# Twelve products of constants on TensorE, ahead of five stages of an attention prologue

## The chip, the cores and the metric

One core of a Trainium2 chip. The metric is the device time of one execution in microseconds (us), taken as the median of the runs. Five engines work side by side and meet through semaphores: PE (matrix products; the trace calls its weight loads PEld), DVE and POOL (elementwise work), ACT (activations and copies) and SP, which here only issues DMAs. Each runs its own instructions strictly in the order in which they were written.

## The reference

Eight batches of 576 tokens, eight heads of 64. Heads 0 to 3 attend to the last 32 tokens, heads 4 to 7 to every 32nd token back. The result, 8 x 576 x 512, goes through a layer norm and a two-layer network of width 2048 with a ReLU, and is added to itself:

```
scores = scale * np.matmul(q, k.transpose(0, 1, 3, 2))
mask_local = (rel >= 0) & (rel < stride)
mask_strided = (rel >= 0) & (pos[None, :] % stride == pos[:, None] % stride)
...
attn = np.exp(scores - np.max(scores, axis=-1, keepdims=True))
attn = attn / (np.sum(attn, axis=-1, keepdims=True) + 1e-09)
x = np.matmul(attn, v) ... reshape(B, S, H * D)
xn = (x - mu) / np.sqrt(var + 1e-06) * g_ln
out = x + np.maximum(xn @ w_ch1, 0.0) @ w_ch2
```

## The kernel before

**Tiling.** The 8 x 576 tokens are cut into nine chunks of 512; chunk c is the first 512 tokens of batch c, and the ninth holds the last 64 of each batch. The network runs chunk by chunk over sixteen slices f of 128 hidden columns. For each slice PE makes a hidden tile `ph` (`ffn1_high` L748 and `ffn1_low` L755, twelve products of 512 columns) and then four output tiles `po` (`ffn2` L775, twelve more), which collect over the slices. Data and weights are each split into a high and a low part, so that three fast products stand for one exact one. Attention runs in pairs of heads and is spread between the slices: while chunk c is in the network, the pairs of batch c + 1 are worked on.

**The prologue** has no chunk to hide behind. It does batch 0 (four pairs), starts batch 1, prepares the sixteen weight slices, and feeds the network of chunk 0 as soon as a slice is ready. Its order is written out by hand in the string `ORDER`, one word for each step, of the form `op:k:i:buf`; `one()` looks the word up and issues the instructions. Since every engine runs in written order, the string is the schedule. The words that matter here, for a pair k:

- `T` (`t_rows`, L371) turns loaded rows of q or k by products with the identity, `c` copies them out on ACT;
- `S` (`s_blocks`, L445) makes the scores, `mask` (L473) and `max` (L486) run on DVE, `sub` (L491) on POOL, `exp` (L497) on ACT;
- `PP` (`p_turn`, L501) turns the weights of attention, `pt` (L506) copies them on ACT, `V` (`v_full`, L515) multiplies by v, `den` and `xo` (L565) divide on DVE;
- `X` (L636) turns the result, `xh` (ACT) and `xl` (DVE) split it; `tp` (L415, L416, L420) turns the q and k of a later pair on DVE.

For a weight slice f: `W` issues its two loads of 512 KB on SP; `low`, `sc`, `mg`, `sg` decode it; `byg` (L270) and `add` (L275, L277) run on POOL, `cm` (L281) is one fp32 product on PE, `cen` (L284) subtracts on DVE; `hi` (L294, ACT) and `lo` (L298, POOL) split it; `F` and `H` are the two halves of `ph`, `Fb` the piece of `F:0` that waits for the last pair, `G` is `po`.

**PSUM.** Each of the prologue's words that needs a PSUM tile takes one of three pairs of banks, named by `buf` (`room()`), and waits there for the reader of the tile before. `ph` has a bank of its own. At the start `wake`, a tile in that bank, receives six products of a constant tile with itself, which nothing reads (L128).

fp32 products other than the turns of `PP` and `X` show in the trace as two records each; the turns and the network's products as one. So `S` of 24 products shows as x48.

Of the kernel before, what the change touches and what calls it, by code (L numbers as in the profile page):

```python
# [20 lines left out]
T:0:0:0 T:0:1:1 c:0:0: c:0:1: T:1:0:2 S:0::0 c:1:0: T:1:1:2 mask:0 max:0 T:2:1:0 c:1:1: sub:0  # L21
S:1::1 c:2:1: exp:0 T:2:0:2 mask:1 max:1 PP:0::0 c:2:0: T:3:0:1 sub:1 pt:0 c:3:0: V:0::2 exp:1
vs:1 S:2::0 den:0 xo:0 PP:1::1 mask:2 X:0::2 pt:1 max:2 W:0 T:3:1:0 xh:0 sub:2 V:1::1 xl:0 c:3:1:
S:3::2 den:1 r:4 xo:1 low:0:0 sc:0:0 low:0:1 exp:2 mg:0:0 mask:3 PP:2::1 X:1::0 pt:2 sg:0:0 W:1
max:3 xh:1 V:2::2 sc:0:1 xl:1 sub:3 tp:4 byg:0 exp:3 W:2 PP:3::0 add:0 den:2 S:4::1 pt:3 mg:0:1
vs:3 xo:2 cm:0::0 low:1:0 X:2::2 W:3 mask:4 sg:0:1 V:3::1 xh:2 max:4 sc:1:0 cen:0 sub:4 xl:2 r:5
hi:0:0 lowA:2:0 mg:1:0 hi:0:1 lo:0:0 F:0 exp:4 den:3 sg:1:0 lowA:3:0 lo:0:1 xo:3 sc:1:1 low:1:1
byg:1 X:3::1 mg:1:1 v:4 sg:1:1 add:1 PP:4::2 xh:3 sc:2:0 xl:3 cm:1::0 mg:2:0 Fb:0 pt:4 lowA:3:1
W:4 cen:1 H:0 lowA:2:1 sg:2:0 hi:1:0 tp:5 byg:2 V:4::0 hh:0 sc:2:1 add:2 hl:0 S:5::1 hi:1:1 st:1
mg:2:1 lo:1:0 cm:2::2 sg:2:1 F:1 W:5 mask:5 sc:3:0 lo:1:1 hi:2:1 cen:2 H:1 mg:3:0 hi:2:0 G:0  # L30
sg:3:0 hh:1 den:4 W:6 sc:3:1 hl:1 lowA:4:1 mg:3:1 lo:2:0 byg:3 lowA:4:0 F:2 sg:3:1 add:3 xo:4
sc:4:0 hi:3:1 W:7 mg:4:0 H:2 lo:2:1 lowA:5:0 sg:4:0 cm:3::0 G:1 cen:3 byg:4 sc:4:1 hi:3:0 mg:4:1
add:4 hh:2 sg:4:1 st:4 hl:2 sc:5:0 X:4::0 lo:3:0 F:3 mg:5:0 xh:4 r:6 lo:3:1 lowA:5:1 xl:4 H:3
sg:5:0 cm:4::0 hh:3 G:2 cen:4 byg:5 sc:5:1 hl:3 lowA:6:1 v:5 add:5 mg:5:1 hi:4:0 sg:5:1 lowA:6:0
lo:4:0 F:4 max:5 sc:6:0 lowA:7:0 mg:6:0 sub:5 lowA:7:1 cm:5::0 sg:6:0 H:4 cen:5 W:8 sc:6:1 byg:6
G:3 hh:4 mg:6:1 add:6 hi:4:1 hl:4 hi:5:0 sg:6:1 lo:5:0 cm:6::0 sc:7:0 F:5 cen:6 W:9 exp:5 lo:4:1
mg:7:0 hi:5:1 sg:7:0 H:5 tp:6 byg:7 sc:7:1 PP:5::0 lowA:8:0 G:4 add:7 st:0 hh:5 hi:6:0 hl:5 lo:5:1
pt:5 r:7 mg:7:1 hi:6:1 S:6::0 lo:6:0 sg:7:1 lowA:9:0 lowA:8:1 F:6 mask:6 sc:8:0 max:6 cm:7::0
mg:8:0 sg:8:0 sub:6 H:6 st:3 G:5 hh:6 cen:7 byg:8 st:2 hl:6 hi:7:0 lo:6:1 tp:7 sc:8:1 hi:7:1
V:5::0 add:8 lowA:9:1 r:8 F:7 mg:8:1 sg:8:1 lo:7:0 den:5 sc:9:0 xo:5 H:7 mg:9:0 sg:9:0 cm:8::0  # L40
hh:7 G:6 exp:6 byg:9 hl:7 W:10 sc:9:1 cen:8 add:9 mg:9:1 hi:8:0 PP:6::0 hi:8:1 sg:9:1 lo:8:0 F:8
tp:8 pt:6 W:11 lo:7:1 hi:9:1 cm:9::0 H:8 lo:8:1 sc:10:0 cen:9 lowA:10:0 G:7 lowA:10:1 mg:10:0 W:12
hi:9:0 sg:10:0 hh:8 byg:10 sc:10:1 hl:8 S:8::0 lowA:11:0 lo:9:0 mg:10:1 F:9 lowA:11:1 sg:10:1 v:6
add:10 mask:8 sc:11:0 H:9 mg:11:0 lo:9:1 lowA:12:1 sg:11:0 cm:10::0 G:8 hh:9 cen:10 byg:11 W:13
sc:11:1 hi:10:0 mg:11:1 hi:10:1 lo:10:0 hl:9 lowA:12:0 S:7::0 sg:11:1 add:11 sc:12:0 F:10 mask:7
W:14 lo:10:1 mg:12:0 cm:11::0 sg:12:0 H:10 max:7 sc:12:1 byg:12 G:9 hh:10 cen:11 st:5 add:12
mg:12:1 hi:11:0 hl:10 lowA:13:1 W:15 lo:11:0 sg:12:1 hi:11:1 cm:12::0 F:11 max:8 sc:13:0 lowA:13:0
cen:12 H:11 mg:13:0 hi:12:0 v:7 sg:13:0 lo:12:0 X:5::0 hh:11 G:10 xh:5 lo:11:1 sc:13:1 xl:5
lowA:14:1 hl:11 sub:7 hi:12:1 mg:13:1 V:6::0 lowA:14:0 r:9 byg:13 F:12 sg:13:1 den:6 add:13 xo:6
sc:14:0 H:12 lo:12:1 lowA:15:0 mg:14:0 exp:7 cm:13::0 sg:14:0 G:11 hi:13:1 cen:13 byg:14 xr:0  # L50
# [14 lines left out]
def kernel(  # L65
# [127 lines left out]
    v_l = [v_local(const.tile([P, 4 * NL, D1], F32, name="v_l")),  # L193
           v_local(early.tile([P, 4 * NL, D1], F32, name="v_l1"))]
    v_s = [v_strided(const.tile([P, 2 * NS, D1], F32, name="v_s")),
           v_strided(early.tile([P, 2 * NS, D1], F32, name="v_s1"))]


# [604 lines left out]
    for p in first:  # L803
        if p.k in BY_DVE:
            p.load_qk(early.tile([P, 2 * S], F32, name=f"raw{p.id}"))
        elif p.k == 0:
            for i in range(2):
                p.load_rows(i, nc.sync, slice(0, 1))
                p.load_rows(i, nc.scalar, slice(1, 2))
        else:  # L810
            p.load_rows(0, nc.sync)
            p.load_rows(1, nc.scalar)
    nc.sync.dma_start(gcol, g_ln.rearrange("(c p) -> p c", p=P))
    for p in first:
        p.load_v(once=True)

# [211 lines left out]
```

## Time and profile before

| | |
|---|---|
| runs | 906.57 us median of 3 (906.55 to 910.79) |
| profiled execution: span from first to last instruction | 907.3 us |
| mean granted TensorE clock over the span | 0.992 |
| PE busy | 884.9 us (98%), 7606 products |
| PEld, DVE, ACT, POOL busy | 728.8, 435.4, 199.7, 147.9 us |
| DMA | 102.98 MB, mean 114 GB/s |

The profiled execution has no time outside its span on record; its span stands 0.7 us above the median of the runs. The page divides the span into 40 slices of 22.7 us; the prologue's first 60 us, with which this document deals, are less than three of them, so the views read below are the timeline and tables of busy time over short windows.

### The profile page before, as it was taken

The page shows a single profiled execution, that of the slowest core. Times are in us where ns is not written, and L with a number is a line of the kernel's source. Part 1 is how long each engine was busy: PE and PEld are TensorE (multiplying, and loading weights), DVE is VectorE, ACT ScalarE, POOL GpSimd, SP SyncE. Part 2 cuts the span into 40 slices and gives each one's busy share as a digit, 9 for nine tenths or more (in the row PEclk, how much of TensorE's full clock was granted, in tenths as well). Part 3 has the DMA queues.
Part 4 walks back from the last instruction along what each step waited for, and adds up shares of the span by engine and source line. Part 5 has one row for each costly group of instructions (what it writes and reads, how often), then busy time and mean ns, then how long its engine had stood idle before and what let it go on. Part 6 is the DMA issues. An engine that isn't in the chain of part 4 may idle for free.

```text
span 907.3 us, 18531 instructions
## 1 busy us (share of the span) xinstructions
PE 884.9 (98%) x7606; PEld 728.8 (80%) x7606; DVE 435.4 (48%) x864; ACT 199.7 (22%) x326; POOL 147.9 (16%) x186
## 2 busy tenths in 40 slices
PE   7699999999999999999999999999999999999997
PEld 6578787888888888888888888888888888888885
DVE  2888877544654455445644464445533321132113
ACT  3477663111111111111111111111111111111110
POOL 5477774000100011000100010001000000000000
PEclk8999999999999999999999999999999999999999
DMA  8887886675867575766666665757443230002001
GB/s 166 226 257 179 247 196 114 147 111 119 134 142 109 102 137 120 124 91 141 109 134 93 135 104 141 100 127 124 116 85 91 49 128 0 1 1 93 0 1 47
DMA packets 339621, 102.98 MB, mean 114 GB/s; under 512 B 276944, under 2 KB 331344, under 8 KB 339536
## 3 DMA queue, kind: packets, MB, share of 16 engines
q1 hardware_dynamic: 249920, 85.53, 42.9%
q10 hardware_dynamic: 89616, 16.26, 11.5%
q8 instruction: 60, 0.98, 0.5%
q14 instruction: 25, 0.20, 0.1%
HBM read 74.02 MB, written 27.72 MB: 112 GB/s over the span
## 4 chain that ended last, share of the span: by engine, by line
PE 93%; DMA 2%; DVE 1%; issue 1%; SPq 1%; POOL 1%; ACT 0%; DVEq 0%; POOLq 0%; ACTq 0%
PE po L775 42%; PE ph L748 28%; PE ph L755 14%; PE m L515 2%; PE m L445 2%; DMA s<-in_moe_w_ch_dram 1%; PE t L371 1%; PE s L445 1%; DMA rows<-in_q_dram 1%; PE av L515 1%; SPq L351 1%; PE cm L281 1%; PE px L636 0%; PE pp L501 0%; POOL r L270 0%
## 5 line engine op out<-in xcount | busy, mean ns | idle before, releaser
L775 PE MATMUL po<-w,hh 128*128 128x512 f32 x1152 | 359.2, 393 | 0.0
L765 DVE SCALAR_TENSOR_TENSOR hl<-ph,hh 128x512 fp32r<-128x512 f32 x144 | 99.3, 690 | 367.0 <-ACT hh L760 367.0
L775 PEld LDWEIGHTS po<-w,hh 128*128 128x128 f32 x1152 | 213.4, 188 | 44.8
L748 PE MATMUL ph<-xh,w 128*128 128x512 f32 x576 | 226.0, 392 | 1.4 <-ACT w L294 1.2
L775 PE MATMUL po<-w,hl 128*128 128x512 f32 x576 | 224.5, 390 | 0.0
L748 PE MATMUL ph<-xl,w 128*128 128x512 f32 x576 | 224.5, 390 | 0.0
L760 ACT ACTIVATE hh<-ph 128x512 fp32r<-128x512 f32 x144 | 86.1, 598 | 483.7 <-PE ph L755 469.0
L755 PE MATMUL ph<-xh,w 128*128 128x512 f32 x576 | 155.3, 392 | 0.0
L748 PEld LDWEIGHTS ph<-xh,w 128*128 128x128 f32 x576 | 108.3, 188 | 24.1 <-ACT w L294 1.4
L775 PEld LDWEIGHTS po<-w,hl 128*128 128x128 f32 x576 | 108.1, 188 | 23.1
L755 PEld LDWEIGHTS ph<-xh,w 128*128 128x128 f32 x576 | 108.2, 189 | 22.5 <-POOL w L298 0.2
L748 PEld LDWEIGHTS ph<-xl,w 128*128 128x128 f32 x576 | 108.3, 188 | 22.0
L491 POOL TENSOR_TENSOR sm<-sm,mx 128x648 f32<-128x648 f32 (+1 forms) x32 | 40.6, 1269 | 440.4 <-DVE mx L486 440.4
L723 POOL TENSOR_TENSOR rs<-rs,mhalf 128x1 f32<-128x1 f32 x36 | 19.7, 548 | 286.5 <-DVE rs L722 286.5
L497 ACT ACTIVATE sm<-sm 128x648 f32<-128x648 f32 (+1 forms) x32 | 23.8, 742 | 104.3 <-POOL sm L491 104.3
L298 POOL TENSOR_TENSOR w<-r,w 128x512 fp32r<-128x512 f32 x32 | 41.1, 1297 | 7.3 <-ACT w L294 6.9
L687 DVE TENSOR_TENSOR xl<-xo,xh 128x512 fp32r<-128x512 f32 x24 | 16.6, 692 | 38.8 <-ACT xh L686 38.8
L686 ACT ACTIVATE xh<-xo 128x512 fp32r<-128x512 f32 x24 | 15.2, 632 | 62.0 <-DMA pd<-sm 18.2
L486 DVE TENSOR_REDUCE mx<-sm 128x12 f32<-128x648 f32 (+1 forms) x32 | 26.3, 822 | 2.1
L565 DVE TENSOR_TENSOR xo<-m,den 64x64 f32<-64x64 f32 (+3 forms) x120 | 27.1, 289 | 0.0
L781 DVE SCALAR_TENSOR_TENSOR x<-po,rs,x 128x512 f32<-128x512 f32 x36 | 24.5, 737 | 2.0 <-PE po L775 1.8
L718 DVE BATCH_NORM_STATS2 st<-x 128x6 f32<-128x512 f32 x36 | 24.3, 674 | 0.0
(95 smaller groups left out, 561.0 us busy)
## 6 DMA issues: line engine op xcount, KB each, us to landing
s<-in_moe_w_ch_dram SPq DMA_DIRECT2D x32, 512.0 KB
out_dram<-x SPq DMA_DIRECT2D x32, 256.0 KB
raw<-in_q_dram SPq DMA_DIRECT2D x112, 72.0 KB
raw<-in_k_dram SPq DMA_DIRECT2D x112, 72.0 KB
xds<-xo SPq DMA_DIRECT2D x32, 162.0 KB
v_l<-in_v_dram SPq DMA_DIRECT2D x32, 144.0 KB
pd<-sm SPq DMA_DIRECT2D x44, 96.0 KB
pt<-pd ACTq DMA_DIRECT2D x44, 96.0 KB
```

The costliest lines, as they stand in the source:

```text
L298: nc.gpsimd.tensor_tensor(out=t[:, 1], in0=self.w[i], in1=t[:, 0].bitcast(F32), op=ALU.subtract)
L445: nc.tensor.matmul(o, lhsT, rhs, start=True, stop=True, tile_position=(64 * h, pos))
L486: nc.vector.reduce_max(mx[:, :, 0:nt], sm, axis=AX.X)
L491: nc.gpsimd.tensor_tensor(out=sm, in0=sm, in1=mx[:, :, 0:nt].unsqueeze(3).broadcast_to([P, 2, nt, sm.shape[3]]), op=ALU.subtract)
L515: nc.tensor.matmul(at(h, t)[m * j:m * (j + 1)], self.p_cols(rows, t, j), self.v[rows, n, 0:w], start=True, stop=True, tile_position=(64 * ...
L565: nc.vector.tensor_tensor(out=xo[r, t0:t1, h0:h1].rearrange("p t h d -> p h t d"), in0=av, in1=den[r, h0:h1, t0:t1].unsqueeze(3).broadcast_to(
L748: nc.tensor.matmul(ph, w1h[:, cc], x[:, cc, :], start=(new and n == 0 and i == 0), stop=False)
L755: nc.tensor.matmul(ph, w1l[:, cc], xt[c][0][:, cc, :], start=False, stop=(cc == NCC - 1))
L760: nc.scalar.activation(out=hh, in_=ph, func=AF.Relu)
L765: nc.vector.scalar_tensor_tensor(out=hl, in0=ph, scalar=0.0, in1=hh.bitcast(F32), op0=ALU.max, op1=ALU.subtract)
L775: nc.tensor.matmul(po[i], hx[:, cs], w, start=(f == 0 and n == 0), stop=(f == NFC - 1 and n == 2))
L781: nc.vector.scalar_tensor_tensor(out=x, in0=po[i], scalar=rs, in1=x, op0=ALU.mult, op1=ALU.add)
```

## The change

The string `ORDER` gets a new word `Z`, five times:

```diff
-T:0:0:0 T:0:1:1 c:0:0: c:0:1: T:1:0:2 S:0::0 ...
+vm R:0:0 R:0:1 R:1:0 R:1:1:1 R:2:0 R:2:1:1 R:3:0 R:3:1:1 g:0 v:0 v:1 v:2 v:3 T:0:0:0 T:0:1:1 c:0:0:
+c:0:1: Z:3 T:1:0:2 S:0::0 ...
...
-xl:1 sub:3 tp:4 byg:0 exp:3 W:2 PP:3::0 add:0 ...
+xl:1 sub:3 tp:4 byg:0 exp:3 W:2 Z:3 PP:3::0 add:0 ...
...
-lo:0:0 F:0 exp:4 den:3 sg:1:0 lowA:3:0 lo:0:1 xo:3 sc:1:1 low:1:1
-byg:1 X:3::1 mg:1:1 v:4 sg:1:1 add:1 PP:4::2 xh:3 sc:2:0 xl:3 cm:1::0 ...
+lo:0:0 Z:2 F:0 exp:4 den:3 sg:1:0 lowA:3:0 lo:0:1 xo:3 sc:1:1 low:1:1 byg:1 Z:2:0:1 X:3::1 mg:1:1
+v:4 sg:1:1 add:1 PP:4::2 xh:3 sc:2:0 xl:3 Z:2:0:1 cm:1::0 ...
...
+        elif op == "Z":
+            t = room(f"d{len(ps)}", buf - 1) if buf else wake
+            for _ in range(k):
+                nc.tensor.matmul(
+                    t[:, 0:2 * P].rearrange("p (n x) -> p n x", x=P), mean,
+                    mean.unsqueeze(1).broadcast_to([P, 2, P]), start=True, stop=True)
```

`Z:3` and `Z:2` write three or two fp32 products of 128 x 256 into `wake`; `Z:2:0:1` writes two into a new tile `d` in the bank pair that `buf` 0 names. Both operands are the constant tile `mean`. Nothing reads the results. In all 12 products: 3 ahead of `T:1:0`, 3 ahead of `PP:3`, 2 ahead of `F:0`, 2 ahead of `X:3`, 2 ahead of `cm:1`.

The rest of the diff gives names to what was written as loops: the first loads (`R`, `g`, `v:0` to `v:3`) and the clearing of the frames of v (`vm`) become words of `ORDER`, and steps take their engine as an argument. On DVE, ACT, POOL and SP the instructions stay the same and in the same order; on PE the twelve products are the only difference.

PE, around `S:4` (`s` from `kt_s`, `qt_s`; `pp` is `PP`, `px` is `X`, `av` is `V`), before:

```order
L501 MATMUL pp_652<-ident,sm_207 128x128 x6
L636 MATMUL px_659<-ident,xo_0_642 128x128 x4
L515 MATMUL av_675<-v_s_204,pt_3_664 64x65 x24
L501 MATMUL pp_712<-ident,sm_208 128x128 x5
L445 MATMUL s_722<-kt_s,qt_s 64x54 x24
L281 MATMUL cm_754<-bsum,mean 128x128
```

and now:

```order
L503 MATMUL pp_655<-ident,sm_195 128x128 x6
L637 MATMUL px_662<-ident,xo_0_645 128x128 x4
L516 MATMUL av_678<-v_s_194,pt_3_667 64x65 x24
L843 MATMUL wake<-mean 128x256 x3
L503 MATMUL pp_718<-ident,sm_196 128x128 x5
L447 MATMUL s_728<-kt_s,qt_s 64x54 x24
L284 MATMUL cm_760<-bsum,mean 128x128
```

The three products stand between `V:2` and `PP:3`, where PE used to go straight on.

PE, from `X:3` to `cm:2` (the `s` here is `S:5`, of a pair of batch 1), before:

```order
L636 MATMUL px_858<-ident,xo_1_852 128x128 x4
L501 MATMUL pp_874<-ident,sm_207 128x128 x6
L281 MATMUL cm_885<-bsum,mean 128x128
L748 MATMUL ph_0_838<-xh_541,w_0_831 128x512
L748 MATMUL ph_0_838<-xl_542,w_0_831 128x512
L755 MATMUL ph_0_838<-xh_541,w_0_831 128x512 x4
L515 MATMUL av_910<-v_s,pt_2_890 64x65 x24
L445 MATMUL s_943<-kt_l,qt_l 32x64 x40
L281 MATMUL cm_990<-bsum,mean 128x128
```

and now:

```order
L843 MATMUL d_866<-mean 128x256 x2
L637 MATMUL px_869<-ident,xo_1_860 128x128 x4
L503 MATMUL pp_885<-ident,sm_195 128x128 x6
L843 MATMUL d_896<-mean 128x256 x2
L284 MATMUL cm_899<-bsum,mean 128x128
L749 MATMUL ph_0_846<-xh_544,w_0_837 128x512
L749 MATMUL ph_0_846<-xl_545,w_0_837 128x512
L756 MATMUL ph_0_846<-xh_544,w_0_837 128x512 x4
L516 MATMUL av_924<-v_s,pt_2_904 64x65 x24
L447 MATMUL s_957<-kt_l,qt_l 32x64 x40
L284 MATMUL cm_1004<-bsum,mean 128x128
```

By the end of this piece PE has twelve products, 24 records in the trace, more behind it than before.

## Rows read from the trace of the kernel before

**Rows 1.** The page's first lines: span; busy us, share, instructions.
```profile
span 907.3 us, 18531 instructions
PE 884.9 (98%) x7606; PEld 728.8 (80%) x7606; DVE 435.4 (48%) x864; ACT 199.7 (22%) x326; POOL 147.9 (16%) x186
```
**Rows 2.** Windows: length, busy us (xcount) by engine, granted PE clock, DMA share, GB/s.
```profile
14.00:15.00 1.00, 0.00 (x0) 0.00 (x0) 0.00 (x0) 0.47 (x1) 0.00 (x0) 0.96 0.45 82
38.00:39.00 1.00, 1.00 (x26) 0.83 (x29) 0.95 (x4) 0.25 (x1) 0.84 (x3) 0.91 1.09 399
49.00:50.00 1.00, 0.57 (x3) 0.58 (x3) 0.90 (x2) 1.00 (x3) 0.37 (x1) 0.53 0.69 155
```
**Rows 3.** Windows of 3 and 5 us, same columns: PE and DVE are columns one and three.
```profile
39.00:42.00 3.00, 3.00 (x54) 2.57 (x56) 3.00 (x5) 0.44 (x1) 2.67 (x3) 0.50 0.58 118
50.00:55.00 5.00, 5.00 (x139) 3.86 (x138) 4.30 (x8) 3.42 (x7) 3.22 (x4) 0.75 1.06 344
```
**Rows 4.** Timeline of PE, 0 to 60 us: start, us, instruction, count [idle before, releaser].
```profile
8.28 1.21 PE L371 MATMUL t<-ident,rows 96*64 96x96 f32 x24 [1.68 <-DMA rows<-in_q_dram]
...
16.28 0.88 PE L445 MATMUL s<-kt_l,qt_l 64*32 64x64 f32 x38 [3.09 <-issue]
...
26.93 0.45 PE L515 MATMUL av<-v_l,pt 64*32 64x65 f32 x28
28.65 0.76 PE L515 MATMUL av<-v_l,pt 64*32 64x65 f32 x52 [1.27 <-issue]
29.21 0.99 PE L445 MATMUL s<-kt_l,qt_l 64*32 64x64 f32 x75
33.03 0.31 PE L445 MATMUL s<-kt_l,qt_l 64*32 64x64 f32 x5 [2.83 <-issue]
...
37.89 0.77 PE L501 MATMUL pp<-ident,sm 128*128 128x128 f32 x5 [1.78 <-ACT sm L497]
38.58 1.40 PE L445 MATMUL s<-kt_s,qt_s 64*64 64x54 f32 x48
...
44.27 0.50 PE L748 MATMUL ph<-xh,w 128*128 128x512 f32 x1 [1.19 <-ACT w L294]
...
46.90 0.63 PE L636 MATMUL px<-ident,xo 128*128 128x128 f32 x4 [0.96 <-DVE xo L565]
...
49.43 0.79 PE L281 MATMUL cm<-bsum,mean 128*128 128x128 f32 x2 [1.24 <-POOL bsum L277]
...
53.49 1.04 PE L445 MATMUL s<-kt_l,qt_l 64*32 64x64 f32 x80
54.46 0.49 PE L281 MATMUL cm<-bsum,mean 128*128 128x128 f32 x2
```
**Rows 5.** The page's DMA queues: the instruction queue: packets, MB, share.
```profile
q8 instruction: 60, 0.98, 0.5%
```
**Rows 6.** The same queue in the window 30.3 to 30.4 us.
```profile
q8 instruction: 1, 0.02, 84.2%
```
**Rows 7.** The same queue in the window 38.8 to 38.9 us.
```profile
q8 instruction: 1, 0.02, 67.2%
```
**Rows 8.** The same queue in the window 56.3 to 56.4 us.
```profile
q8 instruction: 1, 0.02, 67.8%
```
**Rows 9.** Timeline of SP: the first and last of eight weight loads, 47 to 54 us.
```profile
47.77 0.39 SPq L224 DMA_DIRECT2D s<-in_moe_w_ch_dram  x1
...
53.41 0.95 SPq L227 DMA_DIRECT2D s<-in_moe_w_ch_dram  x1
```
**Rows 10.** Timeline of DVE: the mask of S:4, the last turn before S:5.
```profile
40.75 0.82 DVE L473 TENSOR_TENSOR sm<-s,mask_s 128x648 f32<-128x648 f32 x1
...
52.15 0.74 DVE L416 STREAM_TRANSPOSE kt_l<-raw 128x576 f32<-128x576 f32 x1
```
**Rows 11.** The chain that ended last: a product cm at full clock.
```profile
63.13 0.22 PE cm L281 x2
```
**Rows 12.** Timeline of PE, 84 to 180 us: the one idle time in it.
```profile
112.62 0.47 PE L748 MATMUL ph<-xh,w 128*128 128x512 f32 x1 [0.23 <-DMA s<-in_moe_w_ch_dram]
```

More of the change, by code (lines that the diff above doesn't have):

```diff
@@ L20 @@
 ORDER = """
[L21 to L50, printed above, removed]
@@ L59 @@
-ONCE = False
+vm R:0:0 R:0:1 R:1:0 R:1:1:1 R:2:0 R:2:1:1 R:3:0 R:3:1:1 g:0 v:0 v:1 v:2 v:3 T:0:0:0 T:0:1:1 c:0:0:
+c:0:1: Z:3 T:1:0:2 S:0::0 c:1:0: T:1:1:2 mask:0 max:0 T:2:1:0 c:1:1: sub:0 S:1::1 c:2:1: exp:0
+T:2:0:2 mask:1 max:1 PP:0::0 c:2:0: T:3:0:1 sub:1 pt:0 c:3:0: V:0::2 exp:1 vs:1 S:2::0 den:0 xo:0
+PP:1::1 mask:2 X:0::2 pt:1 max:2 W:0 T:3:1:0 xh:0 sub:2 V:1::1 xl:0 c:3:1: S:3::2 den:1 r:4 xo:1
+low:0:0 sc:0:0 low:0:1 exp:2 mg:0:0 mask:3 PP:2::1 X:1::0 pt:2 sg:0:0 W:1 max:3 xh:1 V:2::2 sc:0:1
@@ new lines @@
+xl:1 sub:3 tp:4 byg:0 exp:3 W:2 Z:3 PP:3::0 add:0 den:2 S:4::1 pt:3 mg:0:1 vs:3 xo:2 cm:0::0 low:1:0
+X:2::2 W:3 mask:4 sg:0:1 V:3::1 xh:2 max:4 sc:1:0 cen:0 sub:4 xl:2 r:5 hi:0:0 lowA:2:0 mg:1:0 hi:0:1
+lo:0:0 Z:2 F:0 exp:4 den:3 sg:1:0 lowA:3:0 lo:0:1 xo:3 sc:1:1 low:1:1 byg:1 Z:2:0:1 X:3::1 mg:1:1
+v:4 sg:1:1 add:1 PP:4::2 xh:3 sc:2:0 xl:3 Z:2:0:1 cm:1::0 mg:2:0 Fb:0 pt:4 lowA:3:1 W:4 cen:1 H:0
+lowA:2:1 sg:2:0 hi:1:0 tp:5 byg:2 V:4::0 hh:0 sc:2:1 add:2 hl:0 S:5::1 hi:1:1 st:1 mg:2:1 lo:1:0
@@ new lines @@
+cm:2::2 sg:2:1 F:1 W:5 mask:5 sc:3:0 lo:1:1 hi:2:1 cen:2 H:1 mg:3:0 hi:2:0 G:0 sg:3:0 hh:1 den:4 W:6
+sc:3:1 hl:1 lowA:4:1 mg:3:1 lo:2:0 byg:3 lowA:4:0 F:2 sg:3:1 add:3 xo:4 sc:4:0 hi:3:1 W:7 mg:4:0 H:2
+lo:2:1 lowA:5:0 sg:4:0 cm:3::0 G:1 cen:3 byg:4 sc:4:1 hi:3:0 mg:4:1 add:4 hh:2 sg:4:1 st:4 hl:2
+sc:5:0 X:4::0 lo:3:0 F:3 mg:5:0 xh:4 r:6 lo:3:1 lowA:5:1 xl:4 H:3 sg:5:0 cm:4::0 hh:3 G:2 cen:4
+byg:5 sc:5:1 hl:3 lowA:6:1 v:5 add:5 mg:5:1 hi:4:0 sg:5:1 lowA:6:0 lo:4:0 F:4 max:5 sc:6:0 lowA:7:0
+mg:6:0 sub:5 lowA:7:1 cm:5::0 sg:6:0 H:4 cen:5 W:8 sc:6:1 byg:6 G:3 hh:4 mg:6:1 add:6 hi:4:1 hl:4
@@ new lines @@
+hi:5:0 sg:6:1 lo:5:0 cm:6::0 sc:7:0 F:5 cen:6 W:9 exp:5 lo:4:1 mg:7:0 hi:5:1 sg:7:0 H:5 tp:6 byg:7
+sc:7:1 PP:5::0 lowA:8:0 G:4 add:7 st:0 hh:5 hi:6:0 hl:5 lo:5:1 pt:5 r:7 mg:7:1 hi:6:1 S:6::0 lo:6:0
+sg:7:1 lowA:9:0 lowA:8:1 F:6 mask:6 sc:8:0 max:6 cm:7::0 mg:8:0 sg:8:0 sub:6 H:6 st:3 G:5 hh:6 cen:7
+byg:8 st:2 hl:6 hi:7:0 lo:6:1 tp:7 sc:8:1 hi:7:1 V:5::0 add:8 lowA:9:1 r:8 F:7 mg:8:1 sg:8:1 lo:7:0
+den:5 sc:9:0 xo:5 H:7 mg:9:0 sg:9:0 cm:8::0 hh:7 G:6 exp:6 byg:9 hl:7 W:10 sc:9:1 cen:8 add:9 mg:9:1
@@ new lines @@
+hi:8:0 PP:6::0 hi:8:1 sg:9:1 lo:8:0 F:8 tp:8 pt:6 W:11 lo:7:1 hi:9:1 cm:9::0 H:8 lo:8:1 sc:10:0
+cen:9 lowA:10:0 G:7 lowA:10:1 mg:10:0 W:12 hi:9:0 sg:10:0 hh:8 byg:10 sc:10:1 hl:8 S:8::0 lowA:11:0
+lo:9:0 mg:10:1 F:9 lowA:11:1 sg:10:1 v:6 add:10 mask:8 sc:11:0 H:9 mg:11:0 lo:9:1 lowA:12:1 sg:11:0
+cm:10::0 G:8 hh:9 cen:10 byg:11 W:13 sc:11:1 hi:10:0 mg:11:1 hi:10:1 lo:10:0 hl:9 lowA:12:0 S:7::0
+sg:11:1 add:11 sc:12:0 F:10 mask:7 W:14 lo:10:1 mg:12:0 cm:11::0 sg:12:0 H:10 max:7 sc:12:1 byg:12
+G:9 hh:10 cen:11 st:5 add:12 mg:12:1 hi:11:0 hl:10 lowA:13:1 W:15 lo:11:0 sg:12:1 hi:11:1 cm:12::0
@@ L60 @@
+PP:7::0 lo:14:0 F:14 pt:7 tp:9 st:6 lowA:15:1 add:15 sc:15:1 H:14 r:10 cm:15::0 hh:14 G:13 cen:15
+exp:8 hl:14 hi:14:1 mg:15:1 hi:15:0 sg:15:1 lo:15:0 V:7::0 hi:15:1 xr:3 F:15 lo:15:1 den:7 xo:7
+lo:14:1 xs:2 X:7::0 v:8 H:15 G:14 hh:15 xh:7 hl:15 xl:7 v:9 tp:10 PP:8::0 pt:8 xs:3 st:7 r:11 xs:1
+"""
 EARLY_F0 = True
@@ L191, in v_strided, with v_frames @@
         return t
[L193 to L196, printed above, removed]
+    v_l = [const.tile([P, 4 * NL, D1], F32, name="v_l"),
+           early.tile([P, 4 * NL, D1], F32, name="v_l1")]
+    v_s = [const.tile([P, 2 * NS, D1], F32, name="v_s"),
+           early.tile([P, 2 * NS, D1], F32, name="v_s1")]
+    def v_frames():
+        for t in v_l:
+            v_local(t)
+        for t in v_s:
+            v_strided(t)
     sms = [const.tile([P, NS, 2, 64], F32, name=f"sm{i}") for i in range(2)]
@@ L294, in high, with rest @@
             nc.scalar.activation(out=t[:, 0], in_=self.w[i], func=AF.Copy)
-        def rest(self, i):
+        def rest(self, i, eng):
             t = (w1s, w2s)[i][self.f]
-            nc.gpsimd.tensor_tensor(
+            eng.tensor_tensor(
                 out=t[:, 1], in0=self.w[i], in1=t[:, 0].bitcast(F32), op=ALU.subtract)
@@ L316 @@
     NHP = H // 2
+    CC = 2
     CT = 96
-    NA = S // CT // 2
+    NA = S // (CT * CC)
     n_pair = [0, 0]
@@ L358, in load_rows @@
             if self.rows is None:
-                self.rows = early.tile([CT, 2, 2, NA, 2, D], F32, name=f"rows{self.id}")
+                self.rows = early.tile([CT, 2, 2, NA, CC, D], F32, name=f"rows{self.id}")
             src = (q, k)[i]
@@ L368, in t_rows @@
             for a in range(NA):
-                for c in range(2):
+                for c in range(CC):
                     for h in range(2):
@@ L802 @@
     first = pairs[0:NHP]
[L803 to L815, printed above, removed]
     NP = len(pairs)
@@ L843, in one @@
         p = pairs[k]
-        if op == "T":
+        eng, copy = nc.gpsimd, nc.scalar.copy
+        if op.endswith("D"):
+            op, eng, copy = op[0:-1], nc.vector, nc.vector.tensor_copy
+        if op == "R":
+            if k == 0:
+                p.load_rows(i, nc.sync, slice(0, 1))
+                p.load_rows(i, nc.scalar, slice(1, 2))
+            else:
+                p.load_rows(i, nc.scalar if buf else nc.sync)
+        elif op == "vm":
+            v_frames()
+        elif op == "Z":
[4 more added lines that the diff above has]
+                    mean.unsqueeze(1).broadcast_to([P, 2, P]), start=True, stop=True)
+        elif op == "g":
+            nc.sync.dma_start(gcol, g_ln.rearrange("(c p) -> p c", p=P))
+        elif op == "T":
             p.t_rows(i, room(f"t{k}{i}", buf))
         elif op == "c":
-            p.t_copy(i)
+            p.t_copy(i, copy)
         elif op == "S":
@@ L882, in one @@
         elif op == "v":
-            p.load_v(once=ONCE)
+            p.load_v(once=p.b == 0)
         elif op == "W":
@@ L906, in one @@
         elif op == "lo":
-            split(k).rest(i)
+            split(k).rest(i, eng)
         elif op == "F":
```

50 lines of the change are left out of this document (23 added, 27 removed).

## The prediction

> **What bounds the kernel now.** The page's first lines come first: PE is busy for 98% of 907.3 us [rows 1]. A view of PE alone shows where the rest lies. From 84 to 180 us it has one idle time, 0.23 us at 112.62 [rows 12], and from about 53 us on it works practically without a break; so whatever moves the moment at which PE starts its unbroken run moves the end by as much. The prologue before that moment is where the change lies, and there PE waits for three different things [rows 4]. It waits for other engines (ACT, DVE, POOL) and for the first loads, 0.96 to 1.78 us at a time: these are the five places that get products. It waits three times for "issue", that is, for nothing that the profile shows as work, for 3.09, 1.27 and 2.83 us, each time in the middle of a group of equal products. And its clock falls from the high level (2.4 GHz) to the low one (1.2 GHz). The windows tell when: 1 us with a mean clock of 0.96 from 14 us has the fall at 14.9, 0.91 from 38 us at 38.8, 0.53 from 49 us at 49.1 [rows 2]; the second lasts beyond 42, where the window before it still reads 0.50, and the third to about 52.5, since 0.75 over 50 to 55 is half of it at the low level [rows 3]. Before the first, PE had stopped in the 3.09 us wait for issue; before the second it had waited 1.78 us for ACT; before the third 0.96 us for DVE and then 1.24 us for POOL [rows 4].
>
> **What the products cost.** An fp32 product of 128 columns took 0.22 us at the high clock [rows 11]; one of 256 columns is estimated at twice that, 0.44 us, and 0.88 at the low clock. Ahead of `T:1:0` three (1.3 us) go into 1.68 us of waiting, ahead of `PP:3` three (1.3) into 1.78, ahead of `F:0` two (0.9) into 1.19, ahead of `X:3` two (0.9) into 0.96, ahead of `cm:1` two (0.9) into 1.24 [rows 4]. Each is covered by the wait behind which its stage would stand anyway, so I cost all five at nothing. The tightest cover is the one ahead of `X:3`; if the two ahead of `F:0` ran at the low clock (1.8 us in 1.19), `F:0` and `X:3` would be late by 0.6, of which `cm:1`, held by POOL, gives back 1.24 less 0.88. Between 0 and 0.3 us, then, and I take 0. The two `d` tiles wait for nothing new: the reader of the tile before the first is a DVE step between 42 and 44 us, and the second follows only PE's own.
>
> **What the clock gives back.** The first low stretch stays: nothing is added between the wait for issue at 13.2 us and its end. In the second PE is busy throughout, and half of its time would be saved, some 1.6 us; but DVE is busy for 3.00 of the 3 us from 39 to 42 [rows 3], works through, and it and POOL decide when `F:0` and `cm:1` start (44.27 for ACT's part, 49.43 for POOL's [rows 4]). I take 0. In the third, PE works from 49.43 at the low clock, to 52.5, and at the high one would do the same in half, 1.5 us less: cm, `Fb`, `H`, and then `V:4` and `S:5`. But `S:5` waits for DVE's turn of k, ended at 52.15 + 0.74 = 52.89 [rows 10], where it now starts at 53.49 [rows 4]. So 0.6 us comes through; a bit of DVE's own wait for that cm adds 0.1: **0.7 us gained**, between 0 (the clock falls anyway) and 1.5.
>
> **What the extra instructions move.** A wait for issue that cuts a group of equal products needs a cause, and the page has one: PE's instructions come by DMA, 60 packets of 0.98 MB in all [rows 5], for 7606 products with a weight load each [rows 1], so 254 of these instructions, or about 126 products, to a packet. The waits stand at that distance: from the second to the third 52 + 75 = 127 products [rows 4], from the first to the second 38 and on to 28 over ten groups, 251, two packets. And a packet starts 2.7 us before the third wait ends, 30.3 against 33.03 [rows 6, 4]. So I read it thus: PE holds two packets; it asks for the next when it enters one; if it uses up 126 products before that has come, it stands. The border after the third wait lies behind the 75th record of `S:3`, so by counting on, before the change the next lie in the first records of `V:3` (126 on), in the middle of `V:4` (252) and in `G:0` (378). The packets for the first and the last of these start at 38.8 and 56.3 [rows 7, 8] and are there, by the same 2.7 to 2.9 us, at 41.6 and 59.1; PE needs them at 41.9 and 59.3. It has been just in time, twice.
>
> With the change each border comes earlier in the work, by 6, then 12, then 24 records. Counting the same 126 with `Z` in between, the borders are: 46 of the 48 records of `S:4`; the first record of `V:4`; 78 of the 80 records of `S:5`. The first costs: at the high clock record 46 is reached at 39.4, the packet is there at 41.6, so `S:4` ends at 41.8 instead of 39.98, and DVE's mask, which now starts at 40.75 [rows 10] right behind DVE's step before, starts 1.0 us late. DVE is full there, so `F:0`, `X:3` and `cm:1` are 1.0 us late, `cm:1` at 50.4.
>
> The second border decides. PE enters the packet that begins with `V:4` right behind the last of `H`, which are issued together with `cm:1`: at about 50.6. It holds nothing but the 48 records of `V:4` and 78 of `S:5`, dense little products; the 80 of `S:5` took 1.0 us [rows 4]. With DVE's turn of k 0.8 us late `S:5` starts at 53.7 and comes to its 78th record at 54.7. When is the next packet there? From asking to start it took 1.65 us in one case (28.65 to 30.3 [rows 4, 6]), when little was under way, and 5.8 in another (33.03 to 38.8 [rows 4, 7]), behind weight loads at full rate. The nearest row is the same load stretch: the packet of 56.3, asked for in the middle of `V:4`, before `S:5` starts at 53.49, behind some of the eight weight loads of 512 KB that SP issues from 47.77 to 54.4 [rows 4, 8, 9], while 344 GB/s are moved [rows 3]. Eight loads in 6.6 us is one in 0.8, and one takes 1.5 us at that rate. Asked for at 50.6, an estimated one or two us sooner, the packet has one or two loads fewer ahead of it; I take one, a start at 55.0, between 52.3 (the short delay) and 56.4 (the long one). It is there 2.85 us later, at 57.9, between 55.1 and 59.2. Then come the last two records of `S:5`, and `cm:2`, which now starts at 54.46 [rows 4], starts at 58.0: **3.5 us late**, between 0.7 and 4.8. DVE, which has the mask of `S:5` next, is held as long, and with it the decoding of the weights; nothing is left that would run ahead and give it back. The 0.7 us of the clock and the 1.0 us of `S:4` are not added: both lie before a moment that the packet sets.
>
> **The sum**: 907.3 + 3.5 = 910.8 us of span; the runs' median lies 0.7 below the span, so 910.1 us.
>
> **Rivals.** First, **the packets come in time**, and the clock's gain is what remains. For it: in 60 packets three waits are all that the profile shows, and a packet asked for with little traffic started 1.65 us later; at that pace it would be there at 50.6 + 1.65 + 2.7 = 55.0, when PE needs it at 54.7. Against it: the DMA share is 1.06 from 50 to 55 us [rows 3], and 5.8 us were needed at 33 us under the same load. Time: 907.3 - 0.7 - 0.7 = 905.9 us. It decides from the point where the packet starts before 52 us. The Trainium skill, "Runtime: NRT & Kernel Launch", section Instruction fetch mechanics, says that instructions come in blocks of 256, which agrees with the 254 counted here, and that crossing a block's edge is "mostly hidden"; by that there would be no wait at either border and this rival's 905.9 would hold. This case's trace shows it only in part: three of the first crossings cost 1.27 to 3.09 us.
>
> Second, **the wait for the packet lets the clock fall once more**. For it: it is a wait of over 3 us, and the 3.09 us wait at 13.2 was followed by a low stretch, as were two sums of shorter ones. Against it: the waits of 1.27 and 2.83 us at 27 and 30 us were not. A low stretch of 3.4 us, as from 49.1 to 52.5, does half its work, and PE is the bound by then: 1.7 us more, 911.8, up to 913.
>
> That the products do nothing at all (no clock change, no border moved) has no support: each is on PE's list and takes its records.
>
> **How the numbers follow.** A measurement of this kernel can tell 0.5%, 4.5 us, from no change: below 902.0 is faster, above 911.1 slower. The forecast (910.1, own range 907.3 to 911.4) has 0.45, the packets in time (905.9, 905.0 to 906.6) 0.27, the fall of the clock on top (911.8, 910.3 to 913.1) 0.23; 0.05 is left for the unknown. Slower takes nearly all of the clock rival and the upper edge of the forecast, 0.25; faster has only the unknown, 0.04; the rest, 0.71, is same. The range, 905.2 to 912.6, takes in the first rival but for its best end, and the second up to the last half us.
>
> **What would show it.** Right: a wait for issue that ends near 41.6 with two records of `S:4` behind it, another of 2 to 4 us near 55 with two records of `S:5` behind it, instruction packets starting near 38.8 and 55, `cm:2` near 58, no low clock from 38 to 42. Wrong: `S:5` in one piece and `cm:2` before 54.5 (the first rival), or the mean clock low for 3 us after 58 (the second). If the waits for issue stand at other records than 46 and 78, my count of the borders is wrong, and with it the sum.

## The result, and the profile after

| | before | after |
|---|---|---|
| median of 18 runs each | 906.56 us | 913.41 us |
| lowest to highest | 905.08 to 910.79 | 908.26 to 916.06 |
| profiled execution: span | 907.3 us [rows 1] | 906.4 us (a run of 908.26) |

The ratio is 1.0073, with a 95% interval of 1.0060 to 1.0085: 6.85 us slower, more than the 0.5% that a measurement of this kernel can tell. The forecast of 910.1 had the direction and the place, and about half of the size; 913.41 lies outside the range, 0.8 us above its upper end.

The profiled execution is the fastest of the 18, so it shows where the waits stand, and not how long they are in the usual run. The page's first lines, which answer to [rows 1], have the 24 records more on PE:

```profile
span 906.4 us, 18581 instructions
PE 888.4 (98%) x7630; PEld 731.3 (81%) x7630; DVE 436.2 (48%) x864; ACT 199.9 (22%) x326; POOL 147.7 (16%) x186
```

The timeline of PE in the changed kernel, for [rows 4] (start, us, instruction, count, and in brackets the idle time before and who ended it):

```profile
6.36 1.56 PE L843 MATMUL wake<-mean 128*128 128x256 f32 x6
...
14.54 0.69 PE L447 MATMUL s<-kt_l,qt_l 64*32 64x64 f32 x44 [0.44 <-issue]
...
28.30 0.45 PE L447 MATMUL s<-kt_l,qt_l 64*32 64x64 f32 x11 [3.01 <-issue]
...
32.27 1.56 PE L843 MATMUL wake<-mean 128*128 128x256 f32 x6
...
34.74 0.91 PE L447 MATMUL s<-kt_s,qt_s 64*64 64x54 f32 x46 [0.36 <-DVE den L528]
37.42 0.32 PE L447 MATMUL s<-kt_s,qt_s 64*64 64x54 f32 x2 [1.77 <-issue]
...
40.30 1.90 PE L843 MATMUL wake<-mean 128*128 128x256 f32 x4
...
45.74 1.03 PE L843 MATMUL d<-mean 128*128 128x256 f32 x4
46.91 0.46 PE L284 MATMUL cm<-bsum,mean 128*128 128x128 f32 x2
...
50.10 1.02 PE L447 MATMUL s<-kt_l,qt_l 64*32 64x64 f32 x78 [0.47 <-DVE kt_l L418]
53.30 0.27 PE L447 MATMUL s<-kt_l,qt_l 64*32 64x64 f32 x2 [2.18 <-issue]
53.50 0.49 PE L284 MATMUL cm<-bsum,mean 128*128 128x128 f32 x2
```

Two things are to be seen. `S:4` and `S:5`, which were in one piece before (x48 and x80 [rows 4]), are cut behind record 46 and behind record 78, each by a wait for issue. And up to there the changed kernel is ahead: `S:5` starts at 50.10 instead of 53.49, and 2.18 us of that go into the wait in front of its last two records. Much of this lead is this run's own: its wait in `S:1` is 0.44 us, where the kernel before has 3.09 [rows 4]. The wait in `S:3` has moved by six records (x11 behind it instead of x5 [rows 4]) and is 3.01 us. The first two groups of three products ran at the high clock, 1.56 us each by the timeline, in waits of 1.68 and 1.78 us.

The windows over the same stretches as [rows 2, 3] show the clock (the columns are those of rows 2):

```profile
39.00:42.00 3.00, 3.00 (x85) 2.30 (x84) 3.00 (x6) 2.94 (x6) 1.88 (x2) 0.52 0.95 104
49.00:50.00 1.00, 0.63 (x44) 0.49 (x36) 1.00 (x3) 1.00 (x3) 0.92 (x2) 1.00 1.02 343
50.00:55.00 5.00, 2.72 (x88) 2.25 (x89) 3.25 (x7) 1.66 (x3) 3.54 (x4) 1.00 1.06 372
```

The low stretch from 49.1 to 52.5 is gone (1.00 where 0.53 and 0.75 stood); the one at 39 to 42 us is still there (0.52).

### The profile page after: what moved, and what is told of

It reads as the page before. It is cut to its first block, busy times and chain, and to the rows that moved or that the text cites. A ratio compares the mean times of both kernels' runs of the same rounds, so it can differ in the third digit from the quotient of the medians.

```text
span 906.4 us, 18581 instructions
## 1 busy us (share of the span) xinstructions
PE 888.4 (98%) x7630; PEld 731.3 (81%) x7630; DVE 436.2 (48%) x864; ACT 199.9 (22%) x326; POOL 147.7 (16%) x186
## 3 DMA queue, kind: packets, MB, share of 16 engines
q10 hardware_dynamic: 89616, 16.26, 11.5%
## 4 chain that ended last, share of the span: by engine, by line
PE 92%; DMA 4%; SPq 2%; DVE 1%; issue 0%; ACT 0%; DVEq 0%; ACTq 0%
PE po L776 43%; PE ph L749 29%; PE ph L756 14%; PE m L516 2%; PE m L447 2%; DMA s<-in_moe_w_ch_dram 2%; DMA rows<-in_q_dram 2%; SPq L355 1%; DMA raw<-in_q_dram 0%; DMA v_l<-in_v_dram 0%; PE cm L284 0%; PE av L516 0%; PE px L637 0%; PE pp L503 0%; SPq L230 0%
## 5 line engine op out<-in xcount | busy, mean ns | idle before, releaser
L688 DVE TENSOR_TENSOR xl<-xo,xh 128x512 fp32r<-128x512 f32 x24 | 16.6, 692 | 39.5 <-ACT xh L687 39.5
```

## The experiments

The theory: the time lost is the wait for PE's next instruction packet in `S:5`, which is there because 24 more records move the packet's border, and in the usual run the clock falls behind that wait. Rivals: the products themselves cost the time; or the number of instructions does.

### The two kernels once more, one profile each

> The changed kernel once more, for a second trace. The profiled run of it was the fastest of 18 (908.26 us, median 913.41), so a second one should lie 3 to 6 us higher. Packet theory: the waits for issue stand at the same records again, 46 of 48 in S:4 and 78 of 80 in S:5; what differs from the first trace is how long the waits last (the first wait, in S:1, was 0.44 us there against 3.09 before) and, with them, the clock; cm:2 starts 3 to 6 us later than the 53.50 us of the first trace, by as much as the span is longer. Clock theory: the borders' waits are as short as in the first trace, and the added time lies in products at the low clock.

> The kernel before once more, for a second trace. The span of a run stands about 1.85 us below its time in the result of the changed kernel, so the profiled run of before, with 907.3 us of span, should have been a run of some 909 us, above the median of 906.56. A second trace should show a span near 905, cm:2 starting near 52 us instead of 54.46, and the waits for issue at the same records as before (42 of 80 in S:1, 28 of 80 in V:1, 75 of 80 in S:3), one of them shorter.

Neither is edited. The changed kernel took 915.73 us (span 913.9), the kernel before 909.65 (span 907.9). PE in this trace of the changed kernel:

```profile
16.66 0.94 PE L447 MATMUL s<-kt_l,qt_l 64*32 64x64 f32 x44 [2.57 <-issue]
...
50.95 0.49 PE L284 MATMUL cm<-bsum,mean 128*128 128x128 f32 x2 [0.48 <-POOL bsum L280]
...
54.17 1.02 PE L447 MATMUL s<-kt_l,qt_l 64*32 64x64 f32 x78 [0.47 <-DVE kt_l L418]
58.70 0.37 PE L447 MATMUL s<-kt_l,qt_l 64*32 64x64 f32 x2 [3.52 <-issue]
59.00 0.79 PE L284 MATMUL cm<-bsum,mean 128*128 128x128 f32 x2
```

This run is late from the start: the wait in `S:1` is 2.57 us, where the first trace has 0.44, and the clock is low for some 6 us behind it. Its windows around the wait in `S:5`:

```profile
56.00:58.00 2.00, 0.00 (x0) 0.00 (x0) 0.02 (x1) 1.18 (x2) 1.69 (x2) 0.63 1.05 388
58.00:62.00 4.00, 3.30 (x10) 2.64 (x10) 2.79 (x6) 0.63 (x1) 0.60 (x1) 0.50 1.08 382
62.00:64.00 2.00, 2.00 (x7) 1.55 (x7) 0.29 (x2) 0.00 (x0) 1.92 (x3) 0.66 0.61 227
```

The wait stands at the same records and is 3.52 us; while PE stands, the clock falls (0.63 over 56 to 58, so from 56.5 on), and it stays low to about 63.4 (0.50, then 0.66). PE works from 58.70 at half speed, 4.7 us in which 2.3 are lost.

The second trace of the kernel before is no median run either, as I had expected it to be (a span near 905, `cm:2` near 52). But it stands about as far above its median (3.1 us) as this run of the changed kernel does (2.3), so the two can be compared. Its `cm:1` and `cm:2`:

```profile
50.00 0.79 PE L281 MATMUL cm<-bsum,mean 128*128 128x128 f32 x2 [1.26 <-POOL bsum L277]
...
55.00 0.49 PE L281 MATMUL cm<-bsum,mean 128*128 128x128 f32 x2
```

The comparison splits the difference of the spans, 6.0 us: 0.95 us come from before `cm:1` (50.95 against 50.00), 3.05 from between `cm:1` and `cm:2` (8.05 us instead of 5.00), where the wait lies, together 4.0; 2.0 are left for what follows, 854.9 instead of 852.9 us from `cm:2` to the end, which fits the 2.3 lost at the low clock. I had expected `cm:2` to be later than in the first trace by as much as the span is longer; it is 5.5 us later, and the span 7.5 us longer.

### The borders moved without the products

```diff
-WAKE = 6
+WAKE = 4
...
+    for i in range(14):
+        c = 64 * (i % 2)
+        nc.tensor.matmul(wake[c:c + 64, 0:54], mean[0:64, 0:64], mean[0:64, 0:54],
+                         start=True, stop=True, tile_position=(0, c))
```

This is the kernel before; 14 small products (two records each) replace two of the six at the start, 24 records more in all. Nothing is put into the five waits.

> The kernel before, without any product in a wait: at its start four of the six products of 128 columns are kept and 14 small ones (64 x 64 by 54 columns) added, 24 records more in about the same time, so that every border between instruction packets comes 24 records earlier in the work: 34 of 48 in S:4, before V:4, 79 of 80 in S:5, nearly the borders of the changed kernel. Packet theory: waits for issue at just these records, 2 us or more in S:5, and 910 to 914 us. Clock theory (the change is slower because of what its products do in the waits or to the clock): nothing of it is here, 905.5 to 907.5 us.

912.40 us (910.64 to 915.43, 6 runs), ratio 1.0069 [1.0050, 1.0087], practically the changed kernel's own. The traced run is the slowest of the six, 915.43, as far above their median (3.0 us) as the second trace of the kernel before is above its own. PE, and the windows behind its wait:

```profile
16.26 0.84 PE L449 MATMUL s<-kt_l,qt_l 64*32 64x64 f32 x62 [0.38 <-issue]
...
50.07 0.49 PE L285 MATMUL cm<-bsum,mean 128*128 128x128 f32 x2 [0.70 <-POOL bsum L281]
...
53.28 1.02 PE L449 MATMUL s<-kt_l,qt_l 64*32 64x64 f32 x79 [0.48 <-DVE kt_l L420]
58.20 0.24 PE L449 MATMUL s<-kt_l,qt_l 64*32 64x64 f32 x1 [3.89 <-issue]
58.37 0.49 PE L285 MATMUL cm<-bsum,mean 128*128 128x128 f32 x2
```

```profile
58.00:62.00 4.00, 3.80 (x12) 2.98 (x13) 3.09 (x7) 0.63 (x1) 1.23 (x1) 0.60 0.59 210
62.00:64.00 2.00, 2.00 (x10) 1.66 (x9) 0.13 (x1) 0.76 (x2) 1.84 (x4) 0.94 0.00 0
```

`S:5` is cut one record further on, as the count has it, and the clock is low behind the wait here too: 0.60 over 4 us and 0.94 over 2 are 3.4 us at the low level, 1.7 us lost. Against the second trace of the kernel before, `cm:1` starts at nearly the same moment (50.07 and 50.00), `cm:2` 3.4 us later (58.37 and 55.00), and from there to the end it is 855.3 us instead of 852.9. These two steps, 3.4 and 2.4, are the whole 5.8 us by which the spans differ. The other products at the start are not the cause: the wait in `S:1` ends at 16.26, where it ended at 16.28 before [rows 4]. One expected wait, at record 34 of `S:4`, is not in this trace. The loss needs no product in any wait; the place of the border is enough.

### The waits filled, the borders elsewhere

In the changed kernel one product of 512 columns takes the place of the two or three of 256 (so of 512 or 768 columns), and at the start two of 384 that of the six of 128, so that PE has only a few records more than before:

```diff
-    for _ in range(WAKE):
-        nc.tensor.matmul(wake[:, 0:P], mean, mean, start=True, stop=True)
+    for _ in range(2):
+        nc.tensor.matmul(
+            wake[:, 0:3 * P].rearrange("p (n x) -> p n x", x=P), mean,
+            mean.unsqueeze(1).broadcast_to([P, 3, P]), start=True, stop=True)
...
-            for _ in range(k):
-                nc.tensor.matmul(
-                    t[:, 0:2 * P].rearrange("p (n x) -> p n x", x=P), mean,
-                    mean.unsqueeze(1).broadcast_to([P, 2, P]), start=True, stop=True)
+            nc.tensor.matmul(
+                t[:, 0:4 * P].rearrange("p (n x) -> p n x", x=P), mean,
+                mean.unsqueeze(1).broadcast_to([P, 4, P]), start=True, stop=True)
```

> The changed kernel with a product in each of the five waits, but one of 512 columns in place of two or three of 256 (10 records in place of 24), and the start's six products of 128 columns as two of 384 (4 records in place of 12). With 2 records more than before by S:5, the borders are nearly those of the kernel before: 5 of 80 in V:3, 20 of 48 in V:4, the middle of G:0; none in S:4 or S:5. Packet theory: no wait for issue in S:4 or S:5, 904.5 to 907.5 us. Clock theory: PE is as busy in the waits as in the changed kernel, or nearly, so 911 to 914 us.

906.34 us (904.69 to 909.39, 12 runs), ratio 0.9999 [0.9984, 1.0015]. `S:5` is whole again:

```profile
47.37 0.49 PE L286 MATMUL cm<-bsum,mean 128*128 128x128 f32 x2 [0.47 <-POOL bsum L282]
...
50.59 1.04 PE L449 MATMUL s<-kt_l,qt_l 64*32 64x64 f32 x80 [0.48 <-DVE kt_l L420]
51.71 0.49 PE L286 MATMUL cm<-bsum,mean 128*128 128x128 f32 x2
```

So products in the five waits cost nothing that can be measured here, and they bring nothing that can be measured either.

The opposite, eight records fewer in the kernel before (only the first hunk above), moves the border out of `S:3` into `PP:2`:

> The kernel before with the start's six products of 128 columns as two of 384: 8 records less, so every border lies 8 records later in the work: behind S:3 (3 of 6 in PP:2, where it was 75 of 80 in S:3), 9 of 80 in V:3, 31 of 48 in V:4, in F:2 (was in G:0). Packet theory: S:3 is no longer cut, so DVE's mask of it starts up to 1.3 us earlier (at 32.0 instead of 33.4), and the packet needed in F:2 has 1 to 2 us more to come; 904 to 906.5 us. Rival: no difference, 906 to 907 us.

906.56 us (904.77 to 908.60, 12 runs), ratio 0.9990 [0.9976, 1.0005]: no difference that can be told, as the expectation's rival had it. The wait did not go, it moved with its border, 1.29 us in front of the last three records of `PP:2`:

```profile
28.17 1.03 PE L447 MATMUL s<-kt_l,qt_l 64*32 64x64 f32 x80
...
31.67 0.55 PE L503 MATMUL pp<-ident,sm 128*128 128x128 f32 x3 [1.29 <-issue]
```

### More records still

The kernel before with 60 records more, which puts borders behind record 69 of `V:3` and record 43 of `S:5` (`little(n)` is the loop of small products above):

```diff
-WAKE = 6
+WAKE = 3
...
+    little(14)
...
-T:0:0:0 T:0:1:1 c:0:0: c:0:1: T:1:0:2 ...
+T:0:0:0 T:0:1:1 c:0:0: c:0:1: Y:19 T:1:0:2 ...
...
+        if op == "Y":
+            little(k)
```

> The kernel before with 60 records more, none of them in the change's last four waits: 33 small products (64 x 64 by 54 columns), 14 at the start beside three of its six products of 128 columns and 19 in the wait ahead of T:1:0. Borders now: 3 of 5 in PP:3, 69 of 80 in V:3, 43 of 80 in S:5. Packet theory: more instructions cost less than the 24 of the run with moved borders, because the packet that S:5 needs is now asked for in V:3, some 8 us earlier, when few weight loads are under way; no wait for issue in S:5 over 0.3 us, 904.5 to 907.5 us. Rival (what costs is the number of added instructions): more than the 5.9 us that 24 records cost, 913 us or above.

A miss. 912.99 us (907.06 to 914.21, 12 runs), ratio 1.0041 [1.0021, 1.0061]. The border is where the count puts it, but I had expected its packet early, because PE enters the packet ahead of it already in `V:3`, and it was not:

```profile
41.60 0.33 PE L522 MATMUL av<-v_l,pt 64*32 64x65 f32 x11 [1.17 <-issue]
...
57.42 0.87 PE L452 MATMUL s<-kt_l,qt_l 64*32 64x64 f32 x37 [4.81 <-issue]
58.22 0.79 PE L288 MATMUL cm<-bsum,mean 128*128 128x128 f32 x2
```

The packet started at 55.05, 13.4 us after PE had entered the one before it. A second profile of the same kernel, which took 913.91 us:

> The kernel with 60 records more once more, unchanged, for a second trace. Of its twelve runs three took 907 to 908.2 us and nine 910.7 to 914.2. If the late packet is what makes the nine, a run above 910 shows a wait of over 3 us in S:5 and cm:2 at 57 or later, and a run below 908.5 a wait under 1.5 us there. Rival, the spread has another cause: the wait in S:5 is the same 4 to 5 us in a run of either length.

```profile
55.67 0.87 PE L453 MATMUL s<-kt_l,qt_l 64*32 64x64 f32 x37 [3.55 <-issue]
56.47 0.80 PE L289 MATMUL cm<-bsum,mean 128*128 128x128 f32 x2
```

The wait is again over 3 us (`cm:2` half a microsecond before the 57 expected), so it belongs to this place of the border; no trace of one of the three short runs was caught.

The changed kernel with all its products and 20 small ones more, 64 records more than before:

```diff
-c:0:1: Z:3 T:1:0:2 S:0::0 ...
+c:0:1: Z:3 Y:20 T:1:0:2 S:0::0 ...
```

> The changed kernel with all its twelve products and 20 small products (40 records) more in the wait ahead of T:1:0. Borders: 6 of 48 in S:4, 77 of 80 in V:3, 38 of 80 in S:5. Packet theory: the packet for S:5 is asked for in V:3 and comes in time; a wait for issue stays in S:4, up to 2 us; 904.5 to 908 us, 5 to 8 below the changed kernel. Rival (the products in the waits cost the time): as the changed kernel or slower, 912 to 916 us.

907.46 us (905.65 to 916.45, 12 runs, the second highest 909.33), ratio 1.0005 [0.9984, 1.0025]. It has the most instructions of all, all twelve products, a border in the middle of `S:5`, and no wait there:

```profile
52.28 1.04 PE L453 MATMUL s<-kt_l,qt_l 64*32 64x64 f32 x80 [0.48 <-DVE kt_l L424]
53.41 0.49 PE L290 MATMUL cm<-bsum,mean 128*128 128x128 f32 x2
```

Here the packet started at 45.2, before the loads of 512 KB. With this both rivals fall: neither the products nor the number of instructions costs the time; a packet that isn't there does, with the clock that falls while PE waits for it or just behind.

### The weight loads behind the border

In three kernels the loads of slices 5 to 7, six of 512 KB, go behind `st:4`, to 60 us or later; PE's instructions stay. First the changed kernel:

```diff
-... F:1 W:5 mask:5 ... den:4 W:6 ... add:3 xo:4
-sc:4:0 hi:3:1 W:7 mg:4:0 ... sg:4:1 st:4 hl:2
+... F:1 mask:5 ... den:4 ... add:3 xo:4 st:4 W:5 W:6 W:7
+sc:4:0 hi:3:1 mg:4:0 ... sg:4:1 hl:2
```

> The changed kernel with the loads of weight slices 5, 6 and 7 issued behind the store of pair 4, at 60 us or later instead of 50 to 54, so that fewer loads stand ahead of the packet that S:5 needs. If the packet waits behind weight loads, it starts within 2 us of PE's entry into V:4 (where the two traces of the changed kernel had 3.5 and 5 us), the wait for issue at record 78 of S:5 is below 1 us, and what the late slices cost shows later, as waits of F:5 or of ACT for the loads. If the loads do not matter, the wait is 2 to 3.5 us as before.

Then the same edit in the kernel with the borders moved and no products, and in the one with 60 records more:

> The kernel before with 24 records more at its start and none of the products (borders at record 34 of 48 of S:4 and 79 of 80 of S:5; PE stood 3.89 us in S:5, cm:2 at 58.37), with the weight loads of slices 5 to 7 behind st:4. If these loads make the packet late, the wait in S:5 falls to 1.6 us or less, as it did for the changed kernel (1.58), and cm:2 starts by 56.3. Rival, the products or the moment of asking alone set it: the wait stays between 3 and 4.5 us, cm:2 at 57.5 or later.

> The kernel with 60 records more (borders at record 69 of 80 of V:3 and 43 of 80 of S:5), in which PE stood 4.81 us in S:5 and the packet started at 55.0, 13.4 us after PE had entered the packet before it. Here the weight loads of slices 5 to 7 (six of 512 KB, issued from 51 us there) go behind st:4, at 60 us or later; PE's instructions are the same. If the packet stood behind these loads, it starts between 44 and 52.5 and the wait in S:5 is gone or under 1.5 us. Rival, it is asked for late for a reason that has nothing to do with them: it starts within 1 us of 55.0 and the wait stays at 4 us or more. The time itself says little: the later loads cost something around 72 us, as they did before (about 910 to 918).

The three took 917.56, 917.09 and 921.36 us; the loads are late where their slices are used, PE waiting 3.7 to 5.0 us at 71 to 77 us. What counts is the wait in `S:5`. In this order:

```profile
55.08 0.27 PE L447 MATMUL s<-kt_l,qt_l 64*32 64x64 f32 x2 [1.58 <-issue]
55.28 0.49 PE L284 MATMUL cm<-bsum,mean 128*128 128x128 f32 x2
```

```profile
54.96 0.24 PE L449 MATMUL s<-kt_l,qt_l 64*32 64x64 f32 x1 [0.82 <-issue]
55.13 0.49 PE L285 MATMUL cm<-bsum,mean 128*128 128x128 f32 x2
```

```profile
57.00 0.87 PE L452 MATMUL s<-kt_l,qt_l 64*32 64x64 f32 x37 [4.73 <-issue]
57.80 0.80 PE L288 MATMUL cm<-bsum,mean 128*128 128x128 f32 x2
```

In the first two the wait is shorter: 1.58 where the two traces had 2.18 and 3.52 (I had expected it under 1, with the packet within 2 us of PE's entry into `V:4`; it started 3.5 us behind `cm:1`, where the two traces had 4.0 and 5.3), and 0.82 where it was 3.89. In the third it stays, 4.73 where 4.81 was. What the DMA does suggests why. Windows of the second (the last two columns are DMA share and GB/s), and its instruction queue from 52.4 to 52.8:

```profile
52.00:53.00 1.00, 0.63 (x44) 0.49 (x36) 1.00 (x3) 1.00 (x3) 0.92 (x2) 1.00 0.82 244
53.00:54.00 1.00, 0.88 (x79) 0.86 (x79) 1.00 (x3) 0.81 (x2) 0.92 (x2) 1.00 0.03 12
```

```profile
q8 instruction: 1, 0.02, 15.7%
```

The packet starts as the traffic of the loads issued earlier ends (244 GB/s, then 12). It is the same in the first, whose traffic falls from 242 to 6 GB/s in the same windows and whose packet starts between 52.5 and 53 too, and in the third, later: 342 GB/s over 53 to 54, 131 over 54 to 55, and the packet at 54.56. All three fit loads that hold the packet up. Only the second shows it by its wait, though: a drop of 3.1 us is well over the 1.3 us by which two traces of one kernel differ (2.18 and 3.52, 4.81 and 3.55), the step to 1.58 in the first is not, and there is one trace of each. In the third, where the expectation's rival came true, it would have to be loads issued before 50.6, which I had left where they were. The experiment doesn't tell whether the packet stood behind them for 12 us or was asked for late.

## Why the prediction was right and wrong

**Where the products go, and what they cost.** Right in the sum, nothing. In single places the cover was thinner: in the first trace the two ahead of `F:0` ran at the low clock and took 1.90 us, the "1.8 us in 1.19" of the text, and those ahead of `cm:1` ended at 46.77, 0.3 us behind POOL's `bsum`, which ended at 46.44. The kernel with one product in each wait, ratio 0.9999, and the one with all twelve and 20 more, 1.0005, show no cost that remains.

**What the clock gives back.** The low stretch at 49 us went, as forecast, in both traces. "No low clock from 38 to 42" failed in both: the first has 0.52 over 39 to 42, and in the second the clock is low from 32.6 to 39.5. In the changed kernel none of it reaches the end, since the packet decides later; that too was said. The kernel with one product in each wait has no wait in `S:5` and was no faster either, but its interval, 0.9984 to 1.0015, has room for the 0.7 us of the text.

**The first border** stands at record 46 of 48 as counted. Its price was not 1.0 us: the wait is 1.77 us in the first trace and 0.55 in the second, but DVE, busy till shortly before, lost only 0.34 and 0.20 us at its mask.

**The second border** stands at record 78 of 80 as counted, and the wait there, 2.18 and 3.52 us, is within the 2 to 4 that the text asked for. Forecast were a packet at 55.0, 4.6 us behind `cm:1`, and `cm:2` at 58.0; the traces have packets at 50.9 and 56.2, 4.0 and 5.3 us behind `cm:1`, and `cm:2` at 53.50 and 59.00. The kernel with the borders alone, 1.0069, shows that this border is the loss. The reading under it, that PE asks for a packet on entering the one before, is not shown: in the kernel with 60 records more 13.4 us lay between the two.

**The step that failed.** The sum puts the clock behind the wait at nothing and leaves its fall to a rival: "the fall of the clock on top (911.8, 910.3 to 913.1) 0.23". That rival is what the second trace of the changed kernel has, and the kernel with the borders moved too: 2.3 and 1.7 us of PE's work lost at the low clock, 2.0 and 2.4 us more from `cm:2` to the end. The price of 1.7 was about right, the chance was not. Of the three traces with a border at record 78 or 79 and the loads in their old place only the first, the fastest of 18 runs, is without the fall. The counter-argument, that waits of 1.27 and 2.83 us had not been followed by a fall, took those as the nearest rows. Behind `S:5` the clock was low in the five traces in which the wait was 3.52 to 4.81 us, and high in the three with 0.82 to 2.18. Length alone does not decide it: in the second trace of the kernel before, a wait of 2.01 us in `S:3` was followed by a fall (0.76 over 32 to 33, then 0.50).

The delay itself was nearly right: 3.5 us at `cm:2` in the forecast, 4.0 measured, trace against trace.

**Where the traced run stands.** The text also says: "the runs' median lies 0.7 below the span, so 910.1 us". In every run with both on record the time stands 1.73 to 1.86 us above the span (908.26 and 906.4, 915.73 and 913.9, 909.65 and 907.9 among them). So the profiled execution of the kernel before was a run of about 909.1, 2.5 us over the median, in which PE came late to `cm:2`. If the packet came at a moment of its own, whatever PE does, the median run would lose more than the traced one: its `cm:2` stood at an estimated 51.9 (906.56 less 1.8 less the 852.9 from there to the end in both traces), so a `cm:2` at 58.0 would cost it 6.1 us and not 3.5. The traces do not show that. In the second trace of the changed kernel `cm:1` is 4.0 us later than in the first, and the packet 5.3 us later: it moved with PE. Carried over to the median, the measured 4.0 us and the clock's 2.0 make 906.56 + 4.0 + 2.0 = 912.6. The 0.85 us that are left to the measured 913.41 stay open, since no median run was traced.

The Trainium skill, "Runtime: NRT & Kernel Launch", section Instruction fetch mechanics, calls the crossing of a block's edge "mostly hidden". Most edges here leave no wait in the profile, but that rival's 905.9 did not come: two kernels that differ in a few products at the start, and by them in where the edges lie, stand 1.0069 apart, and a single crossing costs up to 4.81 us.
